# Token and gate of each FFN slot: a line of ranks spread over partitions by DMA and read by VectorE, in place of mask matmuls on TensorE

## The chip, the cores and the metric

One Trainium2 chip, one core. The time is the device time of one execution in microseconds (us), the median of several runs. The profile is one execution taken by the hardware profiler; its span runs from the first to the last instruction. Engines: PE is TensorE's matmul and PEld its weight load, DVE is VectorE, ACT is ScalarE, POOL is GpSimd, SP is SyncE, which here only issues DMAs.

## The reference

Attention with pooled queries, and then a mixture-of-depths FFN on 128 chosen tokens of each batch. Shapes: batch 8, heads 8, sequence 1152, head size 64, so 576 pooled tokens of 512 features; F = 1024; capacity 128; all f32.

```python
q_pool = q.reshape(B, H, S // 2, 2, D).mean(axis=3)
attn = softmax(scale * q_pool @ k.T) @ v            # (B, H, 576, 64)
x = attn.transpose(0, 2, 1, 3).reshape(B, 576, 512)
scores = np.einsum('bsd,d->bs', x, w_gate)
out = x.copy()
for b in range(B):
    top_idx = np.argpartition(-scores[b], capacity)[:capacity]
    xe = x[b, top_idx]
    ye = np.maximum(xe @ w1, 0.0) @ w2
    g = 1.0 / (1.0 + np.exp(-scores[b, top_idx]))
    out[b, top_idx] = x[b, top_idx] + g[:, None] * ye
```

## The kernel before

The work goes in 32 pairs of heads (8 batches of 4), each in two halves of 288 pooled queries: 64 halves. For a half, `scores` (L813) makes nine chunks of transposed scores on TensorE in tiles of 64 x 64, ACT takes the exponential of each into `p` (L820, two buffers), `weighted` (L831) multiplies `p` by the values one half later, ACT copies the result to `two` (L839) and POOL adds its two parts to `av` (L841). `folded` sums the exponentials: POOL adds two thirds of `p` into `acc` (L852), DVE reduces the rest and `acc` (both L857). DVE transposes the next pair's keys and pooled queries (L731, L735), and `av` (L910); POOL pools the queries (L728). The finished `x` of a pair (L951) is stored to the output in memory (L963).

When all four pairs of a batch are there, the generator `routed` chooses tokens and runs the FFN, in pieces between the halves of the following batch. Its method `units` is called once at the end of each half, in program order, and runs every live generator to its next `yield True`. Batch b's first piece is in half 8b + 10. What it does:

- the score line of 576 tokens goes to memory (`row`, L1026) and comes back spread over all 128 partitions (`sc_row`, L1027) and as columns (`gate_sc`, L1028 and L1029), token t * 128 + p in partition p, column t;
- DVE counts for each token how many stand before it, in five column tiles over three halves (L1075, L1084, L1094, into `rank_parts`), and sums that to `rank` (L1111); ACT and POOL make 1 + exp(-score), and DVE its reciprocal, the gate (L1110);
- **slots**: slot i of the FFN is the token of rank i. DVE makes a mask `pick` of rank against slot number (L1116). One half later TensorE multiplies the mask, as five stationary tiles of 128 x 128, by the two columns of `meta`, token row and gate (L1125), and ACT copies the results to `index` and `own_gate` (L1133, L1135);
- POOL gathers the 128 rows of the output with an indirect DMA by `index` into `xe` (L1137). Two halves later TensorE transposes `xe` (L1151), then come both FFN matmuls (L1162, L1175), one per half, the gate as a scale (L1195), the sum (L1198) and an indirect store (L1199).

Batch 6 has one piece less; batch 7 comes after the last half and runs interleaved with the rest of batch 6, piece by piece. Its scores are spread by matmuls, not through memory.

Every engine runs its instructions in the order of the program text. SP's queue holds in an odd half the loads of keys, queries and values for the pair after the next (L703, L706, L717) and the stores of a finished pair (L963), and then whatever the routing pieces of that half issue; it waits in order like the others.

Of the kernel before, what the change touches and what calls it, by code (L numbers as in the profile page):

```python
# [10 lines left out]
P = 128  # L11
# [523 lines left out]
class _Plain:  # L535
# [66 lines left out]
    def constants(self):  # L602
        nc, const = self.nc, self.const
        self.ones = const.tile([P, P], F32, name="ones")
        nc.gpsimd.memset(self.ones[:, :], 1.0)

        once = self.small.tile([1, 1], F32, name="once")
        nc.scalar.activation(once[:, :], self.ones[0:1, 0:1], AF.Exp)

        ps = self.banks()[:, 0, 0:P]  # L610
        for _ in range(12):
            nc.tensor.matmul(ps, lhsT=self.ones[:, :], rhs=self.ones[:, :], start=True, stop=True)
        self.ident = const.tile([P, P], F32, name="ident")
        make_identity(nc, self.ident[:, :])

        self.before = const.tile([P, P], F32, name="before")
        nc.gpsimd.memset(self.before[:, :], 1.0)
        nc.gpsimd.affine_select(
            out=self.before[:, :],
            in_=self.before[:, :],  # L620
            compare_op=ALU.is_gt,
            fill=0.0,
            base=0,
            pattern=[[-1, P]],
            channel_multiplier=1,
        )
        slot_i = self.ffn.tile([P, self.Sp], I32, name="cmp", bufs=1)
        nc.gpsimd.iota(slot_i[:, :], pattern=[[1, self.Sp]], base=0, channel_multiplier=0)
        self.slot_f = const.tile([P, self.Sp], F32, name="slot_f")
        nc.vector.tensor_copy(self.slot_f[:, :], slot_i[:, :])  # L630
        token_i = self.small.tile([P, self.NT], I32, name="token_i")
        nc.gpsimd.iota(token_i[:, :], pattern=[[P, self.NT]], base=0, channel_multiplier=1)
        self.token = const.tile([P, self.NT], F32, name="token")
        nc.vector.tensor_copy(self.token[:, :], token_i[:, :])

        self.same = const.tile([P, BLK], F32, name="same")
        nc.vector.tensor_reduce(
            self.same[:, :],
            self.ident.rearrange("p (g j) -> p j g", j=BLK),
            AX.X,  # L640
            ALU.add,
        )

        self.merge = const.tile([P, P // BLK, BLK], F32, name="merge")
        nc.vector.tensor_copy(
            self.merge[:, :, :], self.same[:, :].unsqueeze(1).broadcast_to([P, P // BLK, BLK])
        )
        self.tiny = const.tile([P, 1], F32, name="tiny")
        nc.gpsimd.memset(self.tiny[:, :], 1e-9)

    def tokens(self):
        nc = self.nc

        self.meta = self.const.tile([P, self.B, self.NT, 2], F32, name="meta")
        for b in range(self.B):
            nc.gpsimd.tensor_scalar(
                out=self.meta[:, b, :, 0],
                in0=self.token[:, :],
                scalar1=float(b * self.Sp),
                scalar2=None,  # L660
                op0=ALU.add,
            )

    def line_of_scores(self):

# [326 lines left out]
    def routed(self, b, part):  # L992
# [73 lines left out]

        parts = ffn.tile([P, NT, 3], F32, name="rank_parts")
        nc.vector.memset(parts[:, :, :], 0.0)
        rank = ffn.tile([P, NT], F32, name="rank")
        for t, rows in tiles:  # L1070
            at = t * P
# [34 lines left out]
        nc.gpsimd.tensor_scalar(  # L1106
            out=gate[:, :], in0=gate[:, :], scalar1=1.0, scalar2=None, op0=ALU.add
        )
        meta = self.meta[:, b, :, :]
        nc.vector.reciprocal(meta[:, :, 1], gate[:, :])  # L1110
        nc.vector.tensor_reduce(rank[:, :], parts[:, :, :], AX.X, ALU.add)  # L1111

        for s0, w in self.slots:

            pick = ffn.tile([P, NT, P], F32, name="pick", bufs=1)
            nc.vector.tensor_tensor(  # L1116
                out=pick[:, :, 0:w],
                in0=self.slot_f[:, s0 : s0 + w].unsqueeze(1).broadcast_to([P, NT, w]),
                in1=rank[:, :].unsqueeze(2).broadcast_to([P, NT, w]),
                op=ALU.is_equal,  # L1120
            )
            yield True
            ps = self.banks()[:, 0, 0:2]
            for t, rows in tiles:
                nc.tensor.matmul(  # L1125
                    ps[0:w, :],
                    lhsT=pick[0:rows, t, 0:w],
                    rhs=meta[0:rows, t, :],
                    start=(t == 0),
                    stop=(t == NT - 1),  # L1130
                )
            index = ffn.tile([P, 1], I32, name="index")
            nc.scalar.copy(index[0:w, :], ps[0:w, 0:1])  # L1133
            own_gate = ffn.tile([P, 1], F32, name="own_gate")
            nc.scalar.copy(own_gate[0:w, :], ps[0:w, 1:2])  # L1135
            xe = ffn.tile([P, self.Dm], F32, name="xe")
            nc.gpsimd.indirect_dma_start(  # L1137
                out=xe[0:w, :],
                out_offset=None,
                in_=rows_out,  # L1140
                in_offset=bass.IndirectOffsetOnAxis(ap=index[0:w, 0:1], axis=0),
                bounds_check=(b + 1) * Sp - 1,
                oob_is_err=False,
            )
            yield True
            yield True

            xeT = ffn.tile([P, self.ND, P], F32, name="xeT")
            pv = self.banks()[:, 0, :].rearrange("p (c n) -> p c n", n=P)
            for c in range(self.ND):  # L1150
                nc.tensor.transpose(  # L1151
                    pv[:, c, 0:w], xe[0:w, c * P : (c + 1) * P], self.ident[0:w, 0:w]
                )
            nc.scalar.copy(xeT[:, :, 0:w], pv[:, 0 : self.ND, 0:w])  # L1154
            yield True

            hT = ffn.tile([P, self.NFC, P], F32, name="hT")
            for f0 in range(0, self.NFC, 4):
                pv = self.banks()[:, 0, :].rearrange("p (c n) -> p c n", n=P)
                for f in range(4):  # L1160
                    for c in range(self.ND):
                        nc.tensor.matmul(  # L1162
                            pv[:, f, 0:w],
                            lhsT=self.w1[:, c, (f0 + f) * P : (f0 + f + 1) * P],
                            rhs=xeT[:, c, 0:w],
                            start=(c == 0),
                            stop=(c == self.ND - 1),
                        )
                    if f == 3:
                        nc.scalar.activation(hT[:, f0 : f0 + 4, 0:w], pv[:, :, 0:w], AF.Relu)  # L1170
                    yield f0 + f == self.NFC - 1

            ps = self.banks()[:, 0, :]
            for f in range(self.NFC):
                nc.tensor.matmul(  # L1175
                    ps[0:w, 0 : self.Dm],
                    lhsT=hT[:, f, 0:w],
                    rhs=self.w2[:, f, :],
                    start=(f == 0),
                    stop=(f == self.NFC - 1),  # L1180
                )
                if f < self.NFC - 1:
                    yield False
            if b == self.B - 1:
                nc.vector.scalar_tensor_tensor(  # L1185
                    out=xe[0:w, :],
                    in0=ps[0:w, 0 : self.Dm],
                    scalar=own_gate[0:w, 0:1],
                    in1=xe[0:w, :],
                    op0=ALU.mult,  # L1190
                    op1=ALU.add,
                )
            else:
                y = ffn.tile([P, self.Dm], F32, name="y", bufs=1)
                nc.scalar.activation(  # L1195
                    y[0:w, :], ps[0:w, 0 : self.Dm], AF.Copy, scale=own_gate[0:w, 0:1]
                )
                nc.gpsimd.tensor_tensor(out=xe[0:w, :], in0=y[0:w, :], in1=xe[0:w, :], op=ALU.add)  # L1198
            nc.gpsimd.indirect_dma_start(  # L1199
                out=rows_out,  # L1200
                out_offset=bass.IndirectOffsetOnAxis(ap=index[0:w, 0:1], axis=0),
                in_=xe[0:w, :],
                in_offset=None,
                bounds_check=(b + 1) * Sp - 1,
                oob_is_err=False,
            )
            yield True

    def counted(self):

        nc, n = self.nc, self.B * self.NPAIR * self.QB
        low = self.small.tile([P, 2], F32, name="low")
        flags = self.ffn.tile([P, n], F32, name="flags", bufs=1)
        for i, (op, bound) in enumerate(((ALU.is_ge, self.LO), (ALU.is_le, self.HI))):
            nc.vector.tensor_scalar(
                out=flags[:, :],
# [198 lines left out]
```

## Time and profile before

Three runs: 721.43, 721.93 and 722.39 us. The profiled execution took 721.9 us with a span of 720.2 us at a granted TensorE clock of 0.997.

| | us | count | mean ns |
|---|---|---|---|
| L831 PE, weighted values | 293.4 | 4608 | 403 |
| L813 PE, scores | 296.1 | 4608 | 405 |
| L820 ACT, exponentials | 319.1 | 576 | 686 |
| L852 POOL, `acc` | 270.2 | 192 | 1436 |
| L857 DVE, folds | 250.8 | 128 | 1960 |
| L1116 DVE, `pick` | 13.1 | 8 | 1635 |
| L1133, L1135 ACT, `index`, `own_gate` | 2.6 | 16 | 163 |
| L1137 POOL, gather | 9.2 | 8 | 1148 |

The page gives busy time by engine and by group of instructions; matmuls are pipelined, so the durations of neighbours overlap and their sum is more than the time TensorE spends on them. The timeline (start, length, engine, line) gives that from one start to the next. A median gather lands 3.7 us after its issue.

### The profile page before, as it was taken

How to read it: one execution, taken by the hardware profiler on the slowest of the kernel's cores; microseconds unless marked ns; L12 is line 12 of the kernel's file. 1: busy time of each engine (PE TensorE's matmuls, PEld its weight loads, DVE VectorE, ACT ScalarE, POOL GpSimd, SP SyncE). 2: the span in 40 equal slices, each digit the busy share in tenths (PEclk: the TensorE clock that was granted, in tenths of full speed). 3: DMA queues.
4: the chain of work that ended last, by engine and by line, in shares of the span. 5: the costliest groups of instructions: out<-in, count | busy, mean ns of one | idle time of the engine just before them, and what ended most of it. 6: DMA issues, size and time to landing. Idle time of an engine off the chain costs nothing. (4 is left out here: it accounts for less than half of the span.)

```text
span 720.2 us, 23525 instructions
## 1 busy us (share of the span) xinstructions
PE 707.6 (98%) x10022; PEld 490.9 (68%) x10022; DVE 495.6 (69%) x763; ACT 444.0 (62%) x976; POOL 483.1 (67%) x451
## 2 busy tenths in 40 slices
PE   8999999999999999999999999999999999999986
PEld 6668887876857667576675767667675676756664
DVE  2877777997359974499744997359863698658540
ACT  5677777767547774576746765477754777556310
POOL 4777877877467874578745797377953879457520
PEclk9999999999999999999999999999999999999998
DMA  8888886888472754655456663746727362611110
GB/s 177 170 169 171 172 157 124 146 144 170 74 145 61 138 101 84 131 93 114 93 106 109 110 125 66 129 87 117 131 66 133 69 125 56 130 20 39 36 33 25
DMA packets 387475, 78.25 MB, mean 109 GB/s; under 512 B 375520, under 2 KB 375520, under 8 KB 387360
## 3 DMA queue, kind: packets, MB, share of 16 engines
q1 hardware_dynamic: 385856, 71.86, 54.3%
q0 software_dynamic: 1280, 4.20, 1.9%
q8 instruction: 81, 1.33, 0.8%
q10 hardware_dynamic: 224, 0.59, 0.3%
q14 instruction: 34, 0.28, 0.1%
HBM read 65.06 MB, written 11.55 MB: 106 GB/s over the span
## 5 line engine op out<-in xcount | busy, mean ns | idle before, releaser
L820 ACT ACTIVATE p<-ps 128x576 f32<-128x576 f32 x576 | 319.1, 686 | 6.1 <-PE ps L813 5.5
L852 POOL TENSOR_TENSOR acc<-p 128x576 f32<-128x576 f32 x192 | 270.2, 1436 | 77.3 <-ACT p L820 73.9
L813 PE MATMUL ps<-qT,kT 64*64 64x288 f32 x4608 | 296.1, 405 | 0.9 <-DVE qT L797 0.7
L831 PE MATMUL ps<-p,v_sb 64*64 64x288 f32 x4608 | 293.4, 403 | 0.0
L831 PEld LDWEIGHTS ps<-p,v_sb 64*64 64x64 f32 x4608 | 202.3, 133 | 78.5 <-ACT p L820 14.3
L813 PEld LDWEIGHTS ps<-qT,kT 64*64 64x64 f32 x4608 | 185.4, 132 | 97.3 <-ACT p L820 19.4
L857 DVE TRANSPOSE_TENSOR_REDUCE fold<-p 128x54 f32<-128x1728 f32 x64 | 126.3, 1974 | 165.7 <-ACT p L820 165.7
L839 ACT COPY two<-ps 128x576 f32<-128x576 f32 x64 | 40.9, 640 | 144.8 <-PE ps L831 120.3
L857 DVE TRANSPOSE_TENSOR_REDUCE fold<-acc 128x54 f32<-128x1728 f32 x64 | 124.5, 1945 | 4.2 <-POOL acc L852 4.0
L841 POOL TENSOR_TENSOR av<-two 128x288 f32<-128x288 f32 x64 | 51.3, 801 | 45.8 <-ACT two L839 45.2
L1162 PEld LDWEIGHTS ps<-xeT,w 128*128 128x128 f32 x512 | 58.0, 192 | 3.7 <-issue 2.6
L1162 PE MATMUL ps<-xeT,w 128*128 128x128 f32 x512 | 59.7, 277 | 0.7 <-ACT xeT L1154 0.7
L951 POOL TENSOR_TENSOR x<-avb,rec 128x576 f32<-128x576 f32 x32 | 37.1, 1159 | 31.6 <-DVE rec L949 16.2
L1175 PE MATMUL ps<-w,hT 128*128 128x512 f32 x128 | 57.1, 598 | 0.0
L920 POOL TENSOR_TENSOR prod<-avb,w_gate 128x288 f32<-128x288 f32 x64 | 51.4, 803 | 0.6 <-DVE avb L910 0.6
L728 POOL TENSOR_TENSOR qp<-qb 128x576 f32<-128x576 f32 x31 | 43.8, 1414 | 1.7 <-DMA qb<-in_q_dram 1.7
L1175 PEld LDWEIGHTS ps<-w,hT 128*128 128x128 f32 x128 | 23.6, 190 | 29.0 <-issue 28.9
L731 DVE STREAM_TRANSPOSE kT<-kb 128x1152 f32<-128x1152 f32 x31 | 42.4, 1368 | 0.0
L1170 ACT ACTIVATE hT<-ps 128x512 f32<-128x512 f32 x16 | 9.6, 598 | 48.7 <-PE ps L1162 48.7
L897 ACT ACTIVATE sums<-total,tiny 32x18 f32<-32x18 f32 x124 | 38.1, 308 | 1.8
L910 DVE STREAM_TRANSPOSE avb<-av 128x288 f32<-128x288 f32 x64 | 29.2, 457 | 13.2 <-POOL av L841 13.2
L1198 POOL TENSOR_TENSOR xe<-y,xe 128x512 f32<-128x512 f32 x7 | 8.9, 1275 | 40.3 <-ACT y L1195 40.3
(84 smaller groups left out, 339.8 us busy)
## 6 DMA issues: line engine op xcount, KB each, us to landing
kb<-in_k_dram SPq DMA_DIRECT2D x124, 144.0 KB, 4.2
qb<-in_q_dram SPq DMA_DIRECT2D x124, 144.0 KB, 4.2
v_sb<-in_v_dram SPq DMA_DIRECT2D x124, 144.0 KB, 3.1
out_dram<-x SPq DMA_DIRECT2D x128, 72.0 KB, 2.4
w<-in_moe_w_dram SPq DMA_DIRECT2D x8, 512.0 KB, 7.9
sc_row<-row SPq DMA_DIRECT2D x7, 288.0 KB
acc<-in_q_dram ACTq DMA_DIRECT2D x2, 288.0 KB
v_sb<-in_v_dram SPq DMA_DIRECT2D x2, 288.0 KB, 5.7
```

Of the source, the lines that this page charges most:

```text
L728: nc.gpsimd.tensor_tensor(out=qp[:, :, :], in0=pair["q"][:, :, 0, :], in1=pair["q"][:, :, 1, :], op=ALU.add)
L731: nc.vector.transpose(kT.rearrange("p (c g i) -> p c g i", c=self.NC, i=BLK), pair["k"].rearrange("p (g c) d -> p c g d", c=self.NC),)
L813: nc.tensor.matmul(sc[keys, j, 0:n], lhsT=pair["kT"][rows, c * P + keys.start : c * P + keys.stop], rhs=pair["qT"][rows, qs], start=True, ...
L820: nc.scalar.activation(p[:, c // G, c % G, :, :], sc[:, :, 0:n], AF.Exp, scale=self.scale)
L831: nc.tensor.matmul(av[j * self.D : (j + 1) * self.D, e, 0:n], lhsT=half["pair"]["v"][keys, j, c, :], rhs=half["p"][keys, c // G, c % G, j, :],
L839: nc.scalar.copy(two[:, :, :], av[:, :, 0:n])
L841: nc.gpsimd.tensor_tensor(out=half["av"][:, :], in0=two[:, 0, :], in1=two[:, 1, :], op=ALU.add)
L852: nc.gpsimd.tensor_tensor(out=acc[:, u, :], in0=units[:, 0, u, :], in1=units[:, 1, u, :], op=ALU.add)
L857: nc.vector.tensor_reduce(fold[:, a, :], of.rearrange("p u (m d) -> p (u m) d", d=BLK), AX.X, ALU.add, apply_transpose=True,)
L920: self.nc.gpsimd.tensor_tensor(out=pair["prod"][:, ns, :], in0=pair["avb"][:, ns, :], in1=self.w_gate[:, hp : hp + 1, :].broadcast_to([P, ...
L1162: nc.tensor.matmul(pv[:, f, 0:w], lhsT=self.w1[:, c, (f0 + f) * P : (f0 + f + 1) * P], rhs=xeT[:, c, 0:w], start=(c == 0), stop=(c == self ...
L1175: nc.tensor.matmul(ps[0:w, 0 : self.Dm], lhsT=hT[:, f, 0:w], rhs=self.w2[:, f, :], start=(f == 0), stop=(f == self.NFC - 1),)
```

## The change

For batches 0 to 6 the mask matmuls, the mask and the two ACT copies are gone. Ranks and gates of all tokens are written as one tile `both` to memory (`row_rank`, 128 partitions of ten numbers) and come back on all partitions as `lines` (128 x 2 x 5 numbers in each, one buffer). One half later, where the matmuls stood, DVE runs two passes over the line: each compares every rank with the partition's own number and sums, once the token numbers (a constant line, `token_line`) and once the gates, where they are equal. POOL adds the batch's first row and gives `index`. Ranks of the 64 places without a token are set to 576. Batch 7 keeps mask and matmuls, with a smaller `meta`. At the start POOL makes the constant line (an iota and a copy), and makes one column of `meta` instead of eight. `flags` of the closing count takes the buffer of `cmp`.

```diff
+        line_i = self.ffn.tile([P, P, 2, self.NT], I32, name="lines", bufs=1)[:, :, 0, :]
+        nc.gpsimd.iota(line_i, pattern=[[1, P], [P, self.NT]], base=0, channel_multiplier=0)
+        self.token_line = const.tile([P, P, self.NT], F32, name="token_line")
+        nc.gpsimd.tensor_copy(self.token_line[:, :, :], line_i)
...
-        self.meta = self.const.tile([P, self.B, self.NT, 2], F32, name="meta")
-        for b in range(self.B):
-            nc.gpsimd.tensor_scalar(
...
+        self.meta = self.const.tile([P, self.NT, 2], F32, name="meta")
+        nc.gpsimd.tensor_scalar(
...
         nc.vector.memset(parts[:, :, :], 0.0)
+
+        nc.vector.memset(parts[self.TAIL :, NF, :], float(Sp))
...
+        if b == self.B - 1:
+            meta = self.meta
+            nc.vector.reciprocal(meta[:, :, 1], gate[:, :])
+            nc.vector.tensor_reduce(rank[:, :], parts[:, :, :], AX.X, ALU.add)
+        else:
+
+            both = ffn.tile([P, 2, NT], F32, name="both")
+            nc.vector.reciprocal(both[:, 1, :], gate[:, :])
+            nc.vector.tensor_reduce(both[:, 0, :], parts[:, :, :], AX.X, ALU.add)
+            row = self.dram.tile([P * 2 * NT], F32, name="row_rank")
+            nc.sync.dma_start(
+                row.rearrange("(p x) -> p x", p=P), both.rearrange("p a t -> p (a t)")
+            )
+            lines = ffn.tile([P, P, 2, NT], F32, name="lines", bufs=1)
+            nc.sync.dma_start(lines.rearrange("p i a t -> p (i a t)"), _rows_of(row[:], P))
...
+            if b == self.B - 1:
+
+                nc.vector.tensor_tensor(
...
+                yield True
+                ps = self.banks()[:, 0, 0:2]
...
+            else:
+                yield True
+
+                found = self.small.tile([P, 1], F32, name="found_token")
+                for of, to in ((self.token_line, found), (lines[:, :, 1, :], own_gate)):
+                    nc.vector.scalar_tensor_tensor(
+                        out=pick.rearrange("p t i -> p (t i)").rearrange("p (i t) -> p i t", t=NT)[0:w],
+                        in0=lines[0:w, :, 0, :],
+                        scalar=self.token[0:w, s0 // P : s0 // P + 1],
+                        in1=of[0:w, :, :],
+                        op0=ALU.is_equal,
+                        op1=ALU.mult,
+                        accum_out=to[0:w, :],
+                    )
+                nc.gpsimd.tensor_scalar(
+                    out=index[0:w, :],
+                    in0=found[0:w, :],
+                    scalar1=float(b * Sp),
+                    scalar2=None,
+                    op0=ALU.add,
+                )
...
-        flags = self.ffn.tile([P, n], F32, name="flags", bufs=1)
+        flags = self.ffn.tile([P, n], F32, name="cmp", bufs=1)
```

More of the change, by code (lines that the diff above doesn't have):

```diff
@@ L652, in tokens @@
         nc = self.nc
-        self.meta = self.const.tile([P, self.B, self.NT, 2], F32, name="meta")
-        for b in range(self.B):
-            nc.gpsimd.tensor_scalar(
[L657 to L662, printed above, removed]
+        self.meta = self.const.tile([P, self.NT, 2], F32, name="meta")
+        nc.gpsimd.tensor_scalar(
+            out=self.meta[:, :, 0],
+            in0=self.token[:, :],
+            scalar1=float((self.B - 1) * self.Sp),
+            scalar2=None,
+            op0=ALU.add,
+        )
     def line_of_scores(self):
@@ L1108, in routed @@
         )
-        meta = self.meta[:, b, :, :]
-        nc.vector.reciprocal(meta[:, :, 1], gate[:, :])
-        nc.vector.tensor_reduce(rank[:, :], parts[:, :, :], AX.X, ALU.add)
+        if b == self.B - 1:
[12 more added lines that the diff above has]
+            nc.sync.dma_start(lines.rearrange("p i a t -> p (i a t)"), _rows_of(row[:], P))
@@ L1113, in routed @@
         for s0, w in self.slots:
             pick = ffn.tile([P, NT, P], F32, name="pick", bufs=1)
[L1116 to L1130, printed above, removed]
-                )
@@ L1132, in routed @@
[L1132 to L1135, printed above, removed]
+            index = ffn.tile([P, 1], I32, name="index")
+            own_gate = ffn.tile([P, 1], F32, name="own_gate")
+            if b == self.B - 1:
+                nc.vector.tensor_tensor(
+                    out=pick[:, :, 0:w],
+                    in0=self.slot_f[:, s0 : s0 + w].unsqueeze(1).broadcast_to([P, NT, w]),
+                    in1=rank[:, :].unsqueeze(2).broadcast_to([P, NT, w]),
+                    op=ALU.is_equal,
+                )
+                yield True
+                ps = self.banks()[:, 0, 0:2]
+                for t, rows in tiles:
+                    nc.tensor.matmul(
+                        ps[0:w, :],
+                        lhsT=pick[0:rows, t, 0:w],
+                        rhs=meta[0:rows, t, :],
+                        start=(t == 0),
+                        stop=(t == NT - 1),
+                    )
+                nc.scalar.copy(index[0:w, :], ps[0:w, 0:1])
+                nc.scalar.copy(own_gate[0:w, :], ps[0:w, 1:2])
+            else:
[10 more added lines that the diff above has]
+                        accum_out=to[0:w, :],
+                    )
+                nc.gpsimd.tensor_scalar(
+                    out=index[0:w, :],
+                    in0=found[0:w, :],
+                    scalar1=float(b * Sp),
+                    scalar2=None,
+                    op0=ALU.add,
+                )
```

## The prediction

> **What bounds the kernel now.** I read the busy shares first, then the groups by line, then TensorE's timeline, then the queue of SyncE. The shares and the slices:
>
> ```profile
> PE 707.6 (98%) x10022; PEld 490.9 (68%) x10022; DVE 495.6 (69%) x763; ACT 444.0 (62%) x976; POOL 483.1 (67%) x451
> PE   8999999999999999999999999999999999999986
> ```
>
> TensorE is busy in 98% of the span and in nine tenths or more of every slice but the ends. DVE, ACT and POOL have about a third of the span free. So time is saved only where TensorE gets less to do, and lost only where TensorE is made to wait. The groups give what the change takes from it (columns: busy us, mean ns, then idle time before it):
>
> ```profile
> L1125 PE MATMUL ps<-meta,pick 128*128 128x2 f32 (+1 forms) x80 | 10.9, 254 | 0.8 <-DVE pick L1116 0.8
> L1125 PEld LDWEIGHTS ps<-meta,pick 128*128 128x128 f32 (+1 forms) x80 | 10.1, 190 | 4.8 <-POOL acc L852 3.1 <-issue 1.6
> ```
>
> 80 matmuls are ten per batch (five tiles, each f32 matmul as two instructions). The 0.8 us wait for `pick` is one case, in batch 7. The durations overlap, so the price must come from the timeline (start, length, line), here for batch 0:
>
> ```profile
> 142.03 4.61 PE L831 MATMUL ps<-p,v_sb 64*64 64x288 f32 x72
> 146.39 4.61 PE L813 MATMUL ps<-qT,kT 64*64 64x288 f32 x72
> 150.77 4.59 PE L831 MATMUL ps<-p,v_sb 64*64 64x288 f32 x72
> 155.30 1.36 PE L1125 MATMUL ps<-meta,pick 128*128 128x2 f32 x10
> 156.59 4.60 PE L813 MATMUL ps<-qT,kT 64*64 64x288 f32 x72
> ```
>
> From the start of L831 to the next L813 an ordinary half takes 146.39 - 142.03 = 4.36 us. With the masks it takes 156.59 - 150.77 = 5.82 us. So **1.46 us of TensorE per batch**: 1.29 us of weight loads and matmuls and 0.17 us at the change of form. Batches 1 to 5 give 1.46 us too, batch 6 gives 1.44.
>
> [...] The trace has 1.28 us for the ten[...]. [...]
>
> ```profile
> L1116 DVE TENSOR_TENSOR pick<-slot_f,rank x8: 824/1750/1755, 152.2 to 691.8; 128x640 f32<-128x640 f32 x8
> ```
>
> (minimum, median, maximum ns). [...] `row` is issued at 361.53 and its reader `sc_row` at 362.88, 1.35 us later.
>
> **The change, part by part.** I follow batch 2, the same as 1 to 5 on TensorE; times are those of before unless marked.
>
> Removed, batches 0 to 6: 7 x 1.46 = 10.2 us of TensorE, on the path. Also DVE's `pick` (1.75 us) and two ACT copies (0.16 and 0.17 us); those engines have room, so nothing is counted.
>
> Moved onto SP: a store and a load, issued at 0.33 us (like `row`) and 0.36 us (like `sc_row`). They stand behind the loads and stores of one pair and ahead of the next pair's:
>
> ```profile
> 312.72 1.73 SPq L717 DMA_DIRECT2D v_sb<-in_v_dram  x4
> 314.55 2.67 SPq L963 DMA_DIRECT2D out_dram<-x  x4
> 317.31 3.76 SPq L703 DMA_DIRECT2D kb<-in_k_dram  x4
> 321.17 3.94 SPq L706 DMA_DIRECT2D qb<-in_q_dram  x4
> 330.23 3.48 SPq L717 DMA_DIRECT2D v_sb<-in_v_dram  x4
> ```
>
> At 317.2 SP now meets the store and waits until DVE has the ranks at 326.95. It issues the store, waits some 1.35 us for it to land, and issues `lines` at 328.4. The keys and queries behind it go from 317.3 to 329.0, so the last query load lands near 341 (8 us of issuing, 4.2 us to land). POOL first reads them at 348.72 (L728): 7 us to spare, nothing charged. The values at 330.23 become 337, and waited for a buffer anyway. Batch 0 meets a full queue: SP gets there at 150.7, DVE at 152.15, so what follows slips by 4 us, and its queries by 4 us of a slack I put at 4 to 8.
>
> `lines` moves 128 x 5,120 B = 640 KB. No row shows it. From below: `gate_sc`, behind the 288 KB `sc_row` on the same queue, landed 3.8 us after `sc_row` was issued. From above: the weight loads of 512 KB take 7.9 us while the DMA engines are 80% busy; by size that is 9.9. [...] I take 6: landed at 334.4.
>
> DVE, one half later: two passes of 640 elements, each with an accumulator read of 0.08 us. Alone 2 x (0.82 + 0.08) = 1.8 us, beside GpSimd 2 x 1.83 = 3.7 us. DVE reaches them after `total` (before: 336.39 + 0.37). Dropping `pick` brings that forward by only some 0.5 us, because `fold<-acc` then waits for POOL's `acc`, which ends at 331.37. So they start at 336.3, when `lines` is there. POOL by then has only the index add left (its `av` ends at 334.25), so I take 1.8: done at 338.1.
>
> POOL: the index add costs 0.24 us (like L1106). The gather starts at 338.6 instead of 334.42, 4.2 us later, and `acc` of the next half behind it slips as much. Who waits? The gather's rows, 3.9 us later at 342.5, go to TensorE's transposes at 349.04 - 1.46 = 347.6: **5 us to spare**. The slipped `acc` ends at 339.8 + 4.15 = 343.9. DVE's next `fold<-acc` waits for it, and the buffer of `p` is written again by ACT near 351.1 - 1.4 = 349.7: 5.8 us to spare. POOL and DVE have 1.5 us and more free in each half and catch up. Charged: 0.
>
> Batch 6, at the end, is tighter. DVE comes to the passes at 664.8, the gather starts near 667.1 and lands at 670.6. TensorE wants it at 672.12 - 1.44 = 670.7. I charge 0.1; as a bound up to 1.4.
>
> Start: an iota (0.62 us for 576 elements at L628, so 0.69) and a copy on POOL (0.46 as a DVE cast, at most 1.6 at GpSimd's two-input rate of 1.41 us per 576). POOL then waits 3.78 us for the queries until 6.51: hidden. Seven fewer L656 instructions (1.6 us) lie ahead of a 3.01 us wait: no gain. The new memset, 8 x 0.07 us on DVE, lies before a 3.36 us wait in batch 7, and in DVE's room elsewhere. `flags` in `cmp`'s buffer: one engine in order, no new wait. Batch 7 keeps its masks.
>
> **Sum.** 720.2 - 10.2 + 0.1 = 710.1 us of span. The profiled run's time of 721.9 stands 1.7 above its span and at the median of the three runs (721.93). So **711.8 us**; from 710.8 (the start and DVE's relief worth something) to 713.3 (batch 6 loses all its gain).
>
> **The rivals.**
> *Given back in part.* The 4.2 us on POOL and DVE surface after all: batches 0 and 6, with the least slack, gain nothing. Then 5 x 1.46 = 7.3 us, 714.6. If the others lose half as well, 3.7 us and 718.2. For it: POOL waits in order, with `acc` and thereby DVE behind it. Against: 5 us of slack at each named consumer.
> *Slower: `lines` lands late.* One broadcast row read 128 times is seen nowhere in this size. DVE waits in order for it, POOL waits for DVE, TensorE for the gather. Counting back from 347.6: gather issued by 343.7, passes begun by 341.5, so `lines` may take 341.5 - 328.4 = 13.1 us before TensorE waits, and 14.6 before the gain is gone. At 17 us each batch loses 2.4: + 17 us, 739. Against: that is twice the time of the slowest 512 KB load in the median, and SP's wait leaves the DMA queue nearly empty.
> *No change: TensorE isn't what the masks cost.* If ACT's exponentials set the rhythm of the half (9 of them, 5.0 us), the gap would only be renamed, at 721.9. Against: ordinary halves without masks run 4.36 + 4.36 us with the same exponentials.
>
> **Chances.** Forecast 0.66; part given back 0.20; no change 0.04; slower 0.10. The range goes from 710.6 up into the second case, to 717.5, which leaves out the rest of it and the other two: under 2 in 10. A measurement here tells about 0.2% (1.4 us) from no change. Faster by more 0.86, within 0.04, slower 0.10.
>
> **What would show it.** Right: L1125 down from 80 to 10 matmuls; L831 to the next L813 at 4.36 us where the masks were; TensorE idle no longer than now; no wait of L1151 for the gather; POOL's index add after an idle of some 4 us that DVE ends; the passes near 0.9 us. Wrong: TensorE waiting at L1151 for `xe` or at L813 for ACT; DVE idle for `lines`; passes of 1.8 us; `kb` or `qb` waited for by DVE or POOL. The weakest step is the landing of `lines`, then batch 6.

## The result, and the profile after

The changed kernel took **712.99 us** (712.13 to 713.91, four runs), the one before 721.68 us beside it (721.23 to 722.39, four runs): a ratio of **0.9879** (95% interval 0.9861 to 0.9897). The forecast was 711.8 us. Line numbers are 4 to 40 higher where the diff has added lines: L817 is `scores` (L813 before), L835 `weighted` (L831), L856 `acc` (L852), L861 the folds (L857), L1177 the gather (L1137), L1191 the transposes of its rows (L1151), L1202 and L1215 the FFN.

Busy shares first, as for the kernel before:

```profile
PE 698.9 (98%) x9952; PEld 493.9 (69%) x9952; DVE 495.7 (70%) x792; ACT 443.1 (62%) x962; POOL 485.9 (68%) x453
PE   8999999999999999999999999999999999999896
```

TensorE lost 70 instructions and 8.7 us of busy time and is as full as before. DVE's busy time is the same: two passes have taken the place of a mask that cost it 1.75 us a batch. The place where the masks stood, on TensorE's timeline (start, length, line), batch 0:

```profile
146.44 4.61 PE L817 MATMUL ps<-qT,kT 64*64 64x288 f32 x72
150.83 4.60 PE L835 MATMUL ps<-p,v_sb 64*64 64x288 f32 x72
155.24 4.55 PE L817 MATMUL ps<-qT,kT 64*64 64x288 f32 x72
```

From L835 to the next L817 it is 4.41 us, where it was 5.82. The step between the two kernels' start times is 1.45 us at each of the seven places, 10.15 in sum. By the masks of batch 7, the last ones left, TensorE is 692.81 - 682.94 = 9.87 us ahead, and 0.20 of the difference went at one place, below.

The substitute, in batch 2 (the number in brackets is the idle time before, with what ended it):

```profile
332.88 0.86 DVE L1160 SCALAR_TENSOR_TENSOR pick<-lines,token,token_line 128x640 f32<-128x640 f32 x1
333.78 0.88 DVE L1160 SCALAR_TENSOR_TENSOR pick<-lines,token 128x640 f32<-128x640 f32 x1
333.83 0.92 POOL L1169 TENSOR_SCALAR index<-found_token 128x1 int32<-128x1 f32 x1 [2.96 <-DVE pick L1160]
335.03 1.14 POOL L1177 DMA_INDIRECT xe<-out_dram,index  x1 [0.28 <-POOL index L1169]
336.20 4.15 POOL L856 TENSOR_TENSOR acc<-p 128x576 f32<-128x576 f32 x3
```

POOL stands for 2.96 us until the first pass has the token numbers, and makes the index beside the second, of which it ends 0.09 us behind. The gather starts 0.71 us ahead of the half's last product, where before it was 5.55 us ahead. The lists of DMA issues (KB each, median us to landing) and of waits (us in total, times, longest) give the rest:

```profile
lines<-row_rank SPq DMA_DIRECT2D x7, 640.0 KB, 4.1
row_rank<-both SPq DMA_DIRECT2D x7, 5.0 KB, 1.4
POOL index L1169 <- DVE pick L1160: 19.5, 7, 3.0
ACT sums L901 <- DVE total L892: 11.4, 6, 2.1
ACT groups L886 <- DVE sum L871: 6.2, 6, 1.2
```

The last wait is not in the profile of before: the copy `groups` is ACT's first work after the exponentials of an even half, and needs DVE's `sum`, which needs POOL's `acc`, which now stands behind the later gather.

**Why the profile shows 8.5 us and not 9.9.** The stretch behind batch 7's masks, in the changed kernel and then in the one before: a window (length, then busy us of PE, PEld, DVE, ACT and POOL, then granted clock, DMA share and GB/s; the window of before takes in its masks too) and TensorE's timeline:

```profile
684.20:689.50 5.30, 5.30 (x9) 2.03 (x8) 0.06 (x2) 0.22 (x2) 1.11 (x1) 0.68 0.18 49
684.21 5.40 PE L1215 MATMUL ps<-w,hT 128*128 128x512 f32 x8
```

```profile
692.50:698.00 5.50, 5.08 (x20) 2.78 (x20) 1.66 (x6) 0.35 (x3) 1.11 (x1) 1.00 0.18 49
694.07 3.70 PE L1175 MATMUL ps<-w,hT 128*128 128x512 f32 x8
```

In this execution TensorE ran at half clock from 684.86 to 688.28, 3.41 us, and the eight L1215 matmuls there took 5.40 us instead of 3.70; up to the next product (L1202, L1162 before) it cost 1.40 us. The kernel before has times of two sorts as well: of its 57 executions measured beside the experiments, 37 had a mean clock of 0.997 or 0.998 and a median span of 720.1, and 20 had 0.996 or less and 721.45. The changed kernel's four were 710.3 and 710.4 at 0.998, 711.7 and 712.0 at 0.996 and 0.995. At like clock **the change is worth 9.6 to 9.75 us in these four executions**. The same kernel measured again, below, had 711.0 and 711.5 at 0.997 and 0.998, and 713.1 and 713.2 at 0.995 and 0.996, so there it is worth 8.25 to 9.1. That a lower mean clock means such a stretch in the tail is seen only where an execution was profiled.

### The profile page after: what moved, and what is told of

It is laid out like the page before. It is cut to its first block, busy times and chain, and to the rows that moved or that the text cites. A ratio compares the mean times of both kernels' runs of the same rounds, so it can differ in the third digit from the quotient of the medians.

```text
span 711.7 us, 23393 instructions
## 1 busy us (share of the span) xinstructions
PE 698.9 (98%) x9952; PEld 493.9 (69%) x9952; DVE 495.7 (70%) x792; ACT 443.1 (62%) x962; POOL 485.9 (68%) x453
## 5 line engine op out<-in xcount | busy, mean ns | idle before, releaser
L856 POOL TENSOR_TENSOR acc<-p 128x576 f32<-128x576 f32 x192 | 265.9, 1413 | 54.3 <-ACT p L824 53.9
L817 PE MATMUL ps<-qT,kT 64*64 64x288 f32 x4608 | 295.9, 405 | 0.9 <-DVE qT L801 0.7
L835 PE MATMUL ps<-p,v_sb 64*64 64x288 f32 x4608 | 293.9, 403 | 0.0
L835 PEld LDWEIGHTS ps<-p,v_sb 64*64 64x64 f32 x4608 | 209.6, 133 | 71.4 <-ACT p L824 14.5
L817 PEld LDWEIGHTS ps<-qT,kT 64*64 64x64 f32 x4608 | 189.7, 132 | 94.7 <-ACT p L824 19.8
L861 DVE TRANSPOSE_TENSOR_REDUCE fold<-p 128x54 f32<-128x1728 f32 x64 | 126.1, 1970 | 128.4 <-ACT p L824 128.4
L861 DVE TRANSPOSE_TENSOR_REDUCE fold<-acc 128x54 f32<-128x1728 f32 x64 | 124.8, 1950 | 39.8 <-POOL acc L856 39.8
L1202 PEld LDWEIGHTS ps<-xeT,w 128*128 128x128 f32 x512 | 58.0, 192 | 3.7 <-issue 2.6
L1202 PE MATMUL ps<-xeT,w 128*128 128x128 f32 x512 | 59.7, 277 | 0.7 <-ACT xeT L1194 0.7
L1215 PE MATMUL ps<-w,hT 128*128 128x512 f32 x128 | 58.8, 612 | 0.0
L901 ACT ACTIVATE sums<-total,tiny 32x18 f32<-32x18 f32 x124 | 38.2, 308 | 13.0 <-DVE total L892 11.4
L1215 PEld LDWEIGHTS ps<-w,hT 128*128 128x128 f32 x128 | 24.2, 194 | 30.1 <-issue 30.0
```

The costliest lines, as they stand in the source:

```text
L817: nc.tensor.matmul(sc[keys, j, 0:n], lhsT=pair["kT"][rows, c * P + keys.start : c * P + keys.stop], rhs=pair["qT"][rows, qs], start=True, ...
L835: nc.tensor.matmul(av[j * self.D : (j + 1) * self.D, e, 0:n], lhsT=half["pair"]["v"][keys, j, c, :], rhs=half["p"][keys, c // G, c % G, j, :],
L856: nc.gpsimd.tensor_tensor(out=acc[:, u, :], in0=units[:, 0, u, :], in1=units[:, 1, u, :], op=ALU.add)
L861: nc.vector.tensor_reduce(fold[:, a, :], of.rearrange("p u (m d) -> p (u m) d", d=BLK), AX.X, ALU.add, apply_transpose=True,)
L1202: nc.tensor.matmul(pv[:, f, 0:w], lhsT=self.w1[:, c, (f0 + f) * P : (f0 + f + 1) * P], rhs=xeT[:, c, 0:w], start=(c == 0), stop=(c == self ...
L1215: nc.tensor.matmul(ps[0:w, 0 : self.Dm], lhsT=hT[:, f, 0:w], rhs=self.w2[:, f, :], start=(f == 0), stop=(f == self.NFC - 1),)
```

## The experiments

### The gain itself: ten matmuls put back

The changed kernel with ten matmuls that nothing reads where the masks stood, once of the masks' form and once with the operands exchanged:

```diff
                 yield True
+                ps = self.banks()[:, 0, :]
+                for t, rows in tiles:
+                    nc.tensor.matmul(
+                        ps[0:w, 0:2], lhsT=self.before[0:rows, :], rhs=self.token[0:rows, 0:2],
+                        start=(t == 0), stop=(t == NT - 1),
+                    )
...
+                        ps[0:2, 0:w], lhsT=self.token[0:rows, 0:2], rhs=self.before[0:rows, :],
```

> The changed kernel with ten mask-like matmuls (128 x 128 stationary, two columns moving) put back at the old place for batches 0 to 6; nothing reads their result. Theory 1 (the gain is TensorE's own time for the masks): 7 x 1.45 = 10.2 us come back, 722.4, and L817 starts 5.8 us after L835 at these places. Theory 2 (the gain came from DVE, ACT or the wait for the mask): they fill gaps, and the time stays at 712 to 714.

> As the run with mask-like matmuls put back, but with the roles turned: two columns stationary, 128 moving; nothing reads the result. If TensorE's price is the loading of 128 columns of weights, little comes back, 0.3 to 0.5 us per batch, 714.5 to 716. If streaming 128 columns costs as much as loading them (L1215 streams 512 in 0.44 us, so 0.11 us for 128), 1.1 to 1.4 us per batch come back, 720 to 722.

Measured: 723.18 us (ratio 1.0016, 1.0008 to 1.0024) and 722.40 us (1.0009, 1.0001 to 1.0017). The whole gain is gone. In the profile with the masks' form TensorE starts every one of the 64 halves within 0.02 us of the kernel before, although the gather still stands 3.4 us later there: the gain is TensorE's time for these ten matmuls, and taking the mask and the two copies off DVE and ACT adds nothing to it. That the median lies 1.2 us above the kernel before is not explained. The second result was not plain from the first. The two timelines at that place, masks' form and exchanged form:

```profile
155.30 1.36 PE L1159 MATMUL ps<-token,before 128*128 128x2 f32 x10
156.60 4.60 PE L817 MATMUL ps<-qT,kT 64*64 64x288 f32 x72
```

```profile
155.31 1.34 PE L1159 MATMUL ps<-before,token 128*2 128x128 f32 x10
156.58 4.59 PE L817 MATMUL ps<-qT,kT 64*64 64x288 f32 x72
```

To load 128 columns and stream two cost what it cost to load two and stream 128: 1.30 and 1.27 us from one start to the next.

### The substitute: what it costs when nothing of it is waited for

The store, the line and the passes are left out; the index is made from a constant and the gate copied from `both`:

> Leaves out the finding of slots for batches 0 to 6: no store of ranks, no spread line, no passes on DVE; the rows gathered are simply the first 128 tokens of the batch with the first gates, so the output differs. Theory 1 (the substitute is hidden but for the 0.2 us that DVE's lag costs at batch 6's score line): 712.0, at most 0.3 us under the changed kernel at equal clock. Theory 2 (the substitute gives back part of the gain all along): 2 us or more faster, under 710.5.

Measured: 712.57 us (0.9866, 0.9849 to 0.9882), spans of 710.0 to 710.6. Without the substitute the kernel is no faster than the changed one at its best (710.3, 710.4). In those executions all of it is hidden: SP's wait, the landing, both passes, the later gather. It is not hidden in every execution: at clocks of 0.997 and 0.998 (0.998 in all four here) the changed kernel measured again had spans of 711.0 and 711.5, 0.4 to 1.5 us more. What was lost there is taken up below.

### How much later may the line come?

The load of `lines` issued twice, or four times, into the same buffer:

```diff
-            nc.sync.dma_start(lines.rearrange("p i a t -> p (i a t)"), _rows_of(row[:], P))
+            for _ in range(2):
+                nc.sync.dma_start(lines.rearrange("p i a t -> p (i a t)"), _rows_of(row[:], P))
```

> The spread of the line is issued twice into the same buffer, the second waiting for the first: it lands some 4.3 us later, near 334 instead of 329.7 in batch 2, a microsecond after DVE is ready for it at 332.9. Slack theory: DVE and POOL wait 1 us longer, TensorE's transposes of the gathered rows still have 4 us, time unchanged within 0.5 us. Rival (what is behind the queue of SyncE or behind POOL has no slack): slower by 1 us per batch, 7 us.

> The spread of the line is issued four times, one after the other: it lands near 342.5 in batch 2 instead of 329.7. Slack theory: passes end at 344.3, the gather is issued at 345.5 and lands 4.4 us later at 349.9, against TensorE's transposes at 344.8: TensorE waits 5 us per batch, 30 to 38 us in all, and waits for the gather. If instead the loads behind it on the queue of SyncE bite first, DVE or POOL wait for keys or queries and TensorE for the transposed keys; if there is far more slack than I count, less than 10 us.

Measured: 721.95 us (1.0006, 0.9988 to 1.0024) and 787.89 us (1.091, 1.0866 to 1.0954). With two loads 9.0 us were lost, where slack would have left the time as it was, and the rival, that what stands behind POOL or SP has none, said 7; with four loads 75 us, twice the 30 to 38 expected. In batch 0 the last of two loads was there at 162.9, 8.6 us after the first issue at 154.3, and with four it took 15.4 us. With one load it takes some 4 us, and DVE comes 6.5 us after the issue. So DVE waits only some 2 us with two loads, 1.5 in the mean of the seven batches, and yet nearly the whole gain is gone: the two profiles, each with one stretch of half clock in the tail, have spans of 720.0 and 711.7. The waits of the kernel with two loads name the way:

```profile
DVE pick L1161 <- DMA lines<-row_rank: 10.4, 7, 2.3
ACT groups L886 <- DVE sum L871: 13.1, 6, 3.2
```

And its timeline, batch 0, one half later:

```profile
172.61 0.33 DVE L871 TENSOR_REDUCE sum<-fold 128x18 f32<-128x108 f32 x1
172.98 0.91 ACT L886 COPY groups<-sum 32x36 f32<-32x36 f32 x4 [3.18 <-DVE sum L871]
173.80 0.62 ACT L843 COPY two<-ps 128x576 f32<-128x576 f32 x1
174.47 0.21 PEld L817 LDWEIGHTS ps<-qT,kT 64*64 64x64 f32 x8 [0.38 <-ACT two L843]
176.47 3.38 PE L817 MATMUL ps<-qT,kT 64*64 64x288 f32 x48 [1.28 <-ACT xeT L1195]
```

The same place in the changed kernel:

```profile
171.02 0.92 ACT L886 COPY groups<-sum 32x36 f32<-32x36 f32 x4 [1.19 <-DVE sum L871]
173.02 0.64 ACT L843 COPY two<-ps 128x576 f32<-128x576 f32 x1 [1.09 <-PE ps L835]
```

In the changed kernel `two` still waits 1.09 us for its product: that is all the slack left. With two loads `sum` comes 1.96 us later, `groups` with it, `two` doesn't wait any more but is waited for, and the FFN's `xeT`, which stands behind it on ACT, holds TensorE for 1.28 us more. The gather's rows, of which I had said that they would decide, weren't waited for in that batch. Nor were the keys and queries that stand behind the second load in SP's queue: DVE and TensorE wait for none of them in the list, and POOL 1.0 us in three times, 0.7 in the changed kernel. With four loads the gather's rows were waited for as well (30.7 us in six times), and the mean clock was 0.951: nine stretches of half clock before the end, seven of which begin within a wait of TensorE of 4 to 10 us or 0.3 us behind it. So its size is not a price of the wait alone.

### The spread of the times: the unaltered kernel, its tail, and the index add

> The changed kernel once more, unaltered. Its four times fall in two pairs, 712.1 and 712.3 at a mean granted clock of 0.998 and 713.7 and 713.9 at 0.995 to 0.996; the profiled one has a stretch of 3.4 us at half clock in the tail (684.9 to 688.3), in the second half of batch 6's last FFN matmuls. Theory 1 (a window of the clock that falls on the quiet stretch around batch 7's masks in some executions): the times again fall near 712.2 or near 713.8, according to the clock, with nothing between. Theory 2 (scatter of memory or queues): times spread without regard to the clock.

The changed kernel again: 714.12 us (0.9889, 0.9873 to 0.9906), spans 711.0 to 713.2. The clock parts the times once more, but both levels lie about 1 us higher than expected, so the clock isn't all of the spread. One of batch 6's last pieces moved ahead of batch 7's masks, so that TensorE has more to do just before them:

```diff
-        pieces(old, self.NFC // 2)
+        pieces(old, self.NFC // 2 + 1)
```

> One more piece of batch 6's last FFN matmuls stands before batch 7's masks (five of eight instead of four), three after. If the half-clock stretch is what costs 1.5 us in some executions, it now meets less work behind the masks and TensorE is busy while it waited for the mask: all times near 712.2, none at 713.8. If the stretch is not the cause, the two levels stay, or the mask matmuls come later by the added piece (0.86 us less the 0.7 us wait) and all times rise by 0.2 to 0.9 us.

Measured: 713.70 us (0.9888, 0.9872 to 0.9905), the profiled one without half clock behind the masks and yet at a span of 712.0. And the index add on DVE, since it took 0.92 us on POOL and not the 0.24 I had counted:

```diff
-                nc.gpsimd.tensor_scalar(
+                nc.vector.tensor_scalar(
                     out=index[0:w, :],
```

> The index add runs on DVE instead of POOL, where it took 0.92 us. The gather starts some 0.9 us earlier and POOL's and DVE's lag shrinks by as much. Slack theory: only the 0.2 us at batch 6's score line comes back, 712.0 at the higher clock, not to be told from the changed kernel. Rival (POOL's lag costs in every batch): 0.9 us per batch, 706.

Measured: 714.05 us (0.9891, 0.9873 to 0.9909). The add takes 0.15 us there, but it comes after the second pass, and the gather starts at the same distance ahead of the last product: on POOL the add had run beside that pass.

None of the three moved the time. But their profiles, set beside each other, show a loss that the first profile of the changed kernel does not have. In `again`, batch 2:

```profile
335.82 1.14 POOL L1177 DMA_INDIRECT xe<-out_dram,index  x1 [0.28 <-POOL index L1169]
337.22 0.64 ACT L843 COPY two<-ps 128x576 f32<-128x576 f32 x1 [2.12 <-PE ps L835]
```

and in the first profile:

```profile
335.03 1.14 POOL L1177 DMA_INDIRECT xe<-out_dram,index  x1 [0.28 <-POOL index L1169]
336.23 0.64 ACT L843 COPY two<-ps 128x576 f32<-128x576 f32 x1 [1.91 <-PE ps L835]
```

The same instruction wakes 1.40 us after the start of the gather instead of 1.20, both times with the product as its releaser. Over batches 0 to 5 of each profiled kernel (worked out from the timelines; the third column is negative where the gather is still running when `two` starts, and the last tells how far TensorE is ahead of the kernel before at the start of the last half):

| kernel | last product's start to `two`, us | gather's end to `two`, us | TensorE ahead, us |
|---|---|---|---|
| before | 0.51 | 4.8 to 4.9 | |
| dead_masks | 0.51 | 1.3 to 1.5 | 0.0 |
| no_finding | 0.49 | 3.6 to 3.8 | 9.7 |
| changed, first profile | 0.49 | -0.1 to 0.1 | 9.8 |
| again | 0.70 to 0.99 | 0.3 to 0.6 | 8.35 |
| tail_split | 0.69 to 0.91 | 0.1 to 0.5 | 8.3 |
| add_on_dve | 0.71 to 1.01 | 0.2 to 0.6 | 8.1 |

Where the gather is long over, `two` is never late. Where the gather ends beside the product, it is late in three executions and not in one. In these three TensorE loses 1.4 to 1.7 us, mostly in the halves where `two` is late, and that accounts for their spans: 713.2 with half clock in the tail as in the first profile's 711.7, and 712.0 twice without it, against 710.3 and 710.4. It isn't the chip alone: dead_masks ran on the same chip as `again` and tail_split, no_finding on that of add_on_dve, and in neither is `two` late.

### The gather moved out of the way

The token's pass and the index add directly behind `sum`, ahead of the next pair's key transpose; the gate's pass stays:

```diff
+                if s == 0:
+                    for find in self.finders:
+                        find()
+                    self.finders = []
                 if s == 0 and loaded:
                     upcoming = loaded
                     self.prepare_pair(upcoming)
```

where `find` is the first pass and the index add, put on the list by `routed` after the load of `lines`.

> The pass that finds the token, and the index add behind it (now on VectorE), stand directly behind VectorE's `sum` of an even half, ahead of the next pair's key transpose; the pass that finds the gate stays where it was. So the gather starts some 2 us earlier (331.5 to 332.5 us in batch 2 instead of 335.0), and it ends about 2 us ahead of the last product of the half before instead of beside it. Theory (what the run after lost beyond its ten matmuls comes from the gather standing late in GpSimd's queue: `groups` on ScalarE waiting for `sum`, `two` waking late, the merge matmul of batch 6): ScalarE's waits for the `sum` and `total` of VectorE go to under 1 us in sum, `two` starts 0.5 us after the last product in every batch, and the time is 712.3 us where no half-clock stretch falls on the tail's second half and 713.9 where one does; the level of 714 or more of the run `again` is not seen, ratio 0.987. Rival A (the late `two` has nothing to do with the gather): it stays late, 0.7 to 1.0 us, and the times keep their spread of 712 to 714. Rival B (the lines come too late for the earlier place): VectorE waits for them 0.5 us or more in most batches, the key transpose slips, and the time is 714 to 716.

> As token_early, and with one of the second product's pieces of batch 6 moved ahead of batch 7's masks (as in tail_split). Theory: both losses are gone together, time 712.0 to 712.6 in every execution, span 710.3 to 710.6, ratio 0.9865. Rival (the two losses have a common cause outside both edits, such as the chip's clock): 713.5 to 714.1, as tail_split and add_on_dve alone.

Measured: 713.83 us (0.9883, 0.9867 to 0.9900) and, with the tail's split, 713.86 us (0.9882, 0.9865 to 0.9898). One part of the theory held: `two` starts 0.49 us after the last product in eleven of the twelve cases (the twelfth waits behind a late `sums`). The other did not: ACT's waits in token_early's profile, which were to go under 1 us, are 24.7 us for `total` and 10.1 for `sum`, where they were 11.4 and 6.2; TensorE is 8.2 us ahead at the last half, not 9.8. Nor did the time follow. Batch 2 of token_early:

```profile
333.11 1.14 POOL L1173 DMA_INDIRECT xe<-out_dram,index  x1 [1.16 <-ACT p L824]
334.28 4.15 POOL L856 TENSOR_TENSOR acc<-p 128x576 f32<-128x576 f32 x3
335.46 4.40 DVE L1263 SCALAR_TENSOR_TENSOR pick<-lines,token 128x640 f32<-128x640 f32 x1
```

The gather now starts 3.7 us ahead of the last product instead of 0.7, POOL's `acc` behind it is as much sooner, and it meets the gate's pass that had been left behind. That pass, which reads two inputs like each `acc`, took 4.40 us instead of 0.88, five times the duration.

Each instruction's start and end look more like a wait than a slower pass, though no run tests it. The pass lasts beyond `acc` (to 338.43) and ends 0.7 us behind `prod`, POOL's next instruction of two inputs (to 339.17); `av`, which comes next, takes 1.39 us instead of 0.79. In the kernel before, the mask `pick` likewise ended 0.7 us behind the first of three `acc`, and the second took 1.99 us instead of 1.41. The index add of the changed kernel ends 0.09 us behind the pass beside it. When a waiting pass gets its turn is open: `pick` let one instruction of POOL go by, the gate's pass four. Either way the two passes took 0.86 and 0.88 us in the changed kernel, where POOL stands for 2.96 us until the first is done, a wait that looks like waste, and the second took 4.40 us where `acc` ran beside it.

The last version keeps both passes together, between the pair's two transposes, with `total` ahead of them and the tail's split:

```diff
+                if h > 1 and s == 0:
+                    of["total"] = self.added(of["groups"])
                 if s == 0 and loaded:
...
         nc.vector.transpose(kT...)
+        self.find_now()
         nc.vector.transpose(qT[:, :], qp.rearrange("p n d -> p (n d)"))
```

> Both passes with the index add between them, all on VectorE, stand together between the next pair's two transposes, and `total` ahead of them; the split of the tail is in it too. In token_early the gather came 2 us sooner, but GpSimd's `acc` came sooner with it and ran beside the gate pass that had been left behind: that pass took 4.40 us instead of 0.88, and `total` and its `sums` on ScalarE came late. Theory (the late `two` belongs to the gather that ends beside it, and what token_early lost belongs to the pass beside `acc`): here the gate pass runs beside the gather only and takes 0.9 us again, the gather ends about 1.3 us ahead of `two`, `two` starts 0.5 us after the last product, ScalarE does not wait for `total`, and the time is 712.0 to 712.6 in every execution (span 710.3 to 710.6), ratio 0.9865. Rival (any place for the passes in VectorE's queue costs some 1.5 us, since what comes behind them slips instead): 713.5 to 714.2.

Measured: 713.39 us (0.9870, 0.9853 to 0.9887); its four spans 710.5, 710.7, 712.3 and 712.5. In its profile, which has no half clock in the tail, everything is as expected; first the gate's pass (minimum, median, maximum ns) and then `two` in batch 2, 0.49 us behind its product though the profile names `acc` as what it waited for:

```profile
L1268 DVE SCALAR_TENSOR_TENSOR pick<-lines,token x7: 875/876/877, 160.9 to 656.5; 128x640 f32<-128x640 f32 x7
```

```profile
336.42 0.64 ACT L844 COPY two<-ps 128x576 f32<-128x576 f32 x1 [1.92 <-POOL acc L857]
```

The pass is short again, `two` starts 0.49 us after the product in all six batches, the list of waits has neither `groups` nor `sums` behind DVE any more, TensorE is 9.8 us ahead at the last half, and the span is 710.5. But two of the four executions had a clock of 0.996 and took 1.8 us more, with the tail's split in place. The split does not keep half clock away: the profile of early_and_split has it from 691.24 to 694.65 us, in batch 7's first FFN product (L1198), which took 9.04 us instead of 7.41, behind waits of 1.18 and 0.67 us; at a mean clock of 0.997, so the mean doesn't betray every such execution. And the version's interval lies on that of the changed kernel: no version here is shown to be faster than the change as made.

Last, the same double load as above, in the kernel with the token's pass early:

> As token_early, with the lines loaded twice, as in lines_x2. VectorE now meets the pass that needs the lines some 2.5 us earlier in its queue, ahead of the next pair's key transpose, so the second load's landing (about 3.3 us later than one alone) holds VectorE itself. Theory (lines_x2 lost its 9 us through VectorE's and GpSimd's queues, by which `sum` of the next half comes late, and not through the gather's landing): as long as GpSimd no longer waits for the pass, the token pass ends at about 334.5 instead of 334.6 us, so the gather comes no later than in the kernel after but VectorE's own work after it slips by 2 to 3 us: 714 to 720 us. Rival (what was lost in lines_x2 came from the second load's traffic itself, which also delays the loads of `kb` and `qb` behind it on SP's queue): 721 to 723, as lines_x2.

Measured: 736.17 us (1.0194, 1.0172 to 1.0216), outside both expectations. Batch 2:

```profile
342.29 0.89 DVE L1264 SCALAR_TENSOR_TENSOR pick<-lines,token,token_line 128x640 f32<-128x640 f32 x1 [3.31 <-DMA lines<-row_rank]
343.40 1.38 DVE L735 STREAM_TRANSPOSE kT<-kb 128x1152 f32<-128x1152 f32 x1
344.70 0.74 DVE L739 STREAM_TRANSPOSE qT<-qp 128x576 f32<-128x576 f32 x1
345.58 0.72 PE L817 MATMUL ps<-qT,kT 64*64 64x288 f32 x8 [0.83 <-DVE qT L739]
```

DVE waits longer (27.8 us in all instead of 10.4), and what now stands behind it is the next pair's `kT` and `qT`, for which TensorE waits, and `total`, for which ACT's `sums` and then `two` wait. The same late load costs 14 us more where the waiting instruction stands further forward in its queue; part of that may be the gate's pass, left behind here as in token_early, where it took 4.40 us beside `acc`. The rival, that the second load's traffic decides, expected 721 to 723; the list has no wait of DVE or TensorE over 0.2 us for a load of keys, queries or values.

## Why the prediction was right, point by point

**The ten matmuls, 1.46 us a batch: right.** It is 1.45 at all seven places, and putting the matmuls back takes the gain away. What of an instruction that time goes to, the load or the stream, is not shown by it: with two columns to load and 128 to stream the ten cost as much (1.27 us from one start to the next, 1.30 the other way round).

**Batch 6, 0.1 us: the size about right by luck, the place wrong.** TensorE waits nowhere for the gathered rows. The 0.20 us go in half 58, where a small matmul (L1019) that merges `line` comes late because DVE's `line` does.

**The line's landing: mis-sized to the safe side.** 4.1 us (3.8 to 4.9 in the four cases that the trace has) against the 6 taken, which was my estimate between the bounds; the lower bound, 3.8 from the smaller spread load, was the good one. The upper one came from the weight loads of 512 KB, 7.9 us in the kernel before. The store took 1.4 us against 1.35 (2.2, 2.1 and 1.8 in batches 0, 1 and 3).

**The passes, 0.9 us each: right.** They took 0.86 and 0.88 us, 1.79 together with their reads. The reason given, that POOL would have little left to do, is stronger than I put it: POOL waits for them, 2.96 us in batch 2. In token_early the same pass beside `acc` took 4.40 us, more than twice the alternative of 1.83 that I had named.

**The index add, 0.24 us: 0.92 measured.** It runs beside the second pass and ends with it. On VectorE it took 0.15 us, and the gather started no sooner.

**The gather 4.2 us later, 5.7 against TensorE: 4.84 measured** (5.55 to 0.71 us ahead of the last product).

**"5 us of slack at each named consumer": wrong, though the sum didn't show it.** I named the transposes of the rows and the buffer of `p`. The nearest consumer was another one, `groups` on ACT, with `two` and the exponentials behind it in ACT's order, and its slack is about 1 us (`two` waits 1.09 us for its product in batch 0). That the sum held in spite of it is partly luck: the gather came 0.7 us ahead of the last product, and in three other profiled executions the same place cost 1.4 to 1.7 us. So the rival "`lines` lands late" was mis-priced as well: not 13.1 us of landing before TensorE waits and 14.6 before the gain is gone, but some 8 us (8.6 in batch 0) with the gain gone already. The landing that I took, 6 us, would have lain just inside the 6.5 to 7.3 us after which DVE comes in batches 0 to 5, and outside the 5.5 of batch 6.

**The start, SP's order: right.** TensorE is 0.05 us behind at most before the first masks, though the iota took 2.04 us and not the 0.69 estimated, and DVE and TensorE wait for no load that they didn't wait for before.

**1.2 us above the forecast.** The two executions at the higher clock, 712.13 and 712.33, are 0.3 to 0.5 us above it, about half in the span (710.3 and 710.4 against 710.1) and half in the time outside it (1.8 to 1.9 us against 1.7). The other 0.8 in the median comes of the two at the lower clock, 1.5 us longer; a third of the executions of the kernel before have that too. In other series the late `two` adds to it. Neither was in my sum: it stands on the span of one profiled execution of before, which had no half clock behind its masks.

**Open.** Why `two` wakes late in some executions where the gather ends beside the product, and in one not, is not shown: the runs show only that with the gather out of the way it doesn't. Where half clock falls in the executions that weren't profiled, and what brings it, is not known either.

## What to carry to other kernels

The step moved here was hidden only up to the nearest consumer of what queues behind it: about 1 us, as `two` waited 1.09 us for its product, and with the load doubled 9.0 us were lost. So follow not the moved result alone, but the next instruction of each queue that it holds up, through every engine that waits for that one in order (here gather, `acc`, `sum`, `groups`, `two`), and take the least slack. Doubling the moved step's slowest part is a cheap test of that slack. And before an engine's wait is taken away as waste, look at what its next instruction will run beside: the gate's pass went from 0.88 to 4.40 us.

## What was not expected of the hardware

- With a stationary tile of two columns and 128 columns streamed, ten f32 matmul instructions took TensorE 1.27 us; with 128 columns stationary and two streamed 1.30 us.
- A VectorE pass with two f32 inputs of 640 elements: 0.83 to 0.89 us in the changed kernel and both_passes_early, where no GpSimd instruction of two inputs ran beside it, 4.40 us in token_early, where it met `acc` and `prod` (two inputs each), while a fold of one input took 1.97 us beside `acc` and 1.98 behind it (changed kernel, 602.67 and 606.55 us). The mask `pick`, of as many elements and inputs, took 1.75 us beside `acc` and 0.82 in batch 7, where GpSimd did nothing. GpSimd's index add on one element per partition: 0.92 us beside such a pass, 0.23 us without (no_finding).
- In the first profile of the changed kernel TensorE's clock was halved for 3.41 us, 0.6 us behind the ten small mask matmuls of batch 7 (1.1 us behind them in `again`, 0.35 in lines_x2, and not at all in add_on_dve). In lines_x4 there were stretches of 3.41, 10.24 and 13.65 us. What sets their place and length was not shown, nor that too little work ahead was the cause: with more work ahead a stretch still came, elsewhere, in early_and_split (691.24 to 694.65 us).
